# One wait instead of two where a matmul unit's row halves change places, with a new work list

## The chip, the cores and the metric

The kernel runs on one core of a Trainium2 chip. The core has five engines that work side by side, each through its own queue in order: TensorE (PE, matmuls; PEld are its weight loads), VectorE (DVE), ScalarE (ACT), GpSimd (POOL) and SyncE (SP). They meet through semaphores. Matmuls write to PSUM, which DVE and ACT can read; all else lives in SBUF, and DMA queues move data between SBUF and memory (HBM). The metric is the device time of one execution in microseconds, the median of the runs of one kernel.

## The reference

Attention over 8 batches of 8 heads, 576 queries each, with 16 extra "beacon" keys in front that every query sees; the other keys are causal. Its output, as 4608 tokens of 512, goes through a SwiGLU feed-forward block with an inner width of 1536.

```python
k_all = np.concatenate([beacon_k, k], axis=2)          # 592 keys, D = 64
v_all = np.concatenate([beacon_v, v], axis=2)
scores = scale * np.matmul(q, k_all.transpose(0, 1, 3, 2))
scores = np.where(causal, -1000000000.0, scores)
a = np.exp(scores - scores.max(-1, keepdims=True))
a /= a.sum(-1, keepdims=True) + 1e-09
attn_out = np.matmul(a, v_all)                          # (8, 8, 576, 64)
x = attn_out.transpose(0, 2, 1, 3).reshape(4608, 512)
g = x @ w_gate
silu = g * (1.0 / (1.0 + np.exp(-g)))
out = silu * (x @ w_val) @ w_out
```

All inputs and the output are float32; the kernel casts to bf16 as it loads and multiplies in bf16 with float32 sums.

## The kernel before

**Two row halves.** Most matmuls contract over 64 rows only. The array's 128 rows are used as two halves: two matmuls with 64 rows each run at the same time, one in rows 0 to 63, the other in rows 64 to 127, and they write to two different PSUM banks. A unit is one PSUM tile of two banks. In a gate/value unit, for example, rows 0 to 63 first sum the gate into bank 0 while rows 64 to 127 sum the value into bank 1 (piece G, four pairs of matmuls); then the halves change places, rows 64 to 127 finish the gate and rows 0 to 63 the value (piece H, four pairs). Attention-value units (P, then p, 15 pairs each) and projections (24 pieces F of one pair each, of which the first twelve have the first order) do the same. [...] The function `halves` (L112 to L134) issues every such matmul and decides on the wait: it keeps, for each bank of a PSUM slot, the row half that wrote it last, that matmul's name, its place in the order, and a flag that says whether a wait is still owed. A wait is an instruction on TensorE's queue that depends on an earlier matmul; in the built program it hangs on the next weight load. Whatever follows on TensorE stands behind it. With `last` as the latest matmul in either bank of the slot, the test is:

```python
if last[3]:
```

After a wait all flags of the slot are cleared; the matmul issued next sets its own bank's flag. So the first matmul of the new order (rows 64 to 127, bank 0) waits for the last one of the old order, and its partner (rows 0 to 63, bank 1) finds the flag that the first has just set and waits for that one in turn.

**The work list.** There is no loop over the work. A string, `plan` (L610 to L629), names the pieces in the order in which they are issued; each letter calls one function with its own running count (`piece`, L544 to L597), and as every engine takes its queue in order, the string fixes the order on each of them. The letters that matter here:

- `l`: the next load from the list `loads` (L525 to L539), issued on POOL's queue. A load waits until the one eight places earlier has landed, and until its buffer is free. Four loads are issued ahead of the list.
- `c C 0`, `T`, `K k Q q`: for batches 0 to 2, regrouping, transposes on TensorE and copies of k and q; `t`: for batches 3 to 7, a DMA transpose on SP's queue.
- `S` and `s`: scores of one of four parts (A, B, C, D) of a head pair; `s` also adds the causal mask by matmuls. `E`: exponent on ACT.
- `M`, `D`: the causal mask of the next unit that `s` didn't mask, on POOL (L329, an affine select) or on DVE (L325, a product).
- `P`, `p`, `R`: attention-value in both orders, and the division on DVE. The P of a head pair reads the masked exponents of its four parts.
- `X`, `V`: transposes of x, on TensorE for batch 0 and as DMA on SP's queue for the others.
- `g`: the first gate/value unit, in pieces that `parts` (L541) lists; `G`, `H`: the other 107 units. `a`, `1`, `2`: tanh on ACT (L413) and two DVE steps (L417, L424), of which the last frees the PSUM slot.
- `F`: one pair of a projection; `O`, `o`: its copy on DVE or ACT, with the store on SP's queue. `h`, `b`: a few warming matmuls, and a copy of the first beacons.

There are four PSUM slots of two banks (`take`, `give`), taken and given back in turn by scores, attention-value, gate/value units, projections and transposes.

Of the kernel before, what the change touches and what calls it, by code (L numbers as in the profile page):

```python
# [55 lines left out]
def kernel(  # L56
# [55 lines left out]
    def halves(key, bank, row, o, l, r, start, stop, turn=False):  # L112

        at = (held[key], bank)
        was = writers.get(at)
        if was is not None and was[0] != row:
            last = max((w for (i, _), w in writers.items() if i == at[0]), key=lambda w: w[2])
            if last[3]:
                gate = nc.tensor.nop()
                tc.add_manual_dep(  # L120
                    gate.ins,
                    last[1],
                    mybir.DependencyInfo(mybir.DependencyClass.Sync, mybir.DependencyReason.DATA),
                    reason="one bank, two row halves",
                )
            for other, w in writers.items():
                if other[0] == at[0]:
                    writers[other] = (w[0], w[1], w[2], False)
        if turn:
            ins = nc.tensor.transpose(o, l, r)  # L130
        else:
            ins = nc.tensor.matmul(o, lhsT=l, rhs=r, start=start, stop=stop)  # L132
        order[0] += 1
        writers[at] = (row, ins.ins.name, order[0], True)  # L134
# [94 lines left out]
    def turn(n):  # L229
        b, m = divmod(n, NPAIR)  # L230
        t_ps = turned[n] = take(("t", n), [P, 2, 1024], BF16, "t_ps")
        g = grouped.pop(n)
        for i in range(ROWS):
            for row in range(2):
                r = slice(HALF * row, HALF * row + HALF)
                halves(("t", n), row, row, t_ps[:, row, HALF * i : HALF * i + HALF], g[r, i, :], ident[r, r], 1, 1, True)
        if m == 0:
            for mm in range(NPAIR):
                halves(
                    ("t", n), 0, 0, t_ps[:, 0, S + HALF * mm : S + HALF * mm + HALF],  # L240
                    beacons[:, b, P * mm : P * mm + P], ident[0:HALF, 0:HALF], 1, 1, True,
                )
# [19 lines left out]
    def dma_transposes(b):  # L262
        def one(is_k, c, n):
            nc.sync.dma_start_transpose(
                (qT, kT)[is_k][b % 2][:, :, P * c : P * c + n],
                qk[b % 2][0:n, QK * is_k + H * D * c : QK * is_k + H * D * c + H * D],
            )

        todo = []
        for c in range(NKT):  # L270
            todo.append(lambda c=c: one(1, c, P if c < 4 else 80))
            todo.append(lambda c=c: one(0, c, P if c < 4 else 64))
        return todo
# [8 lines left out]
    def scores(n, masked):  # L282
        b, m, u = unit(n)
        ps = take(("s", n), [P, 2, 512], FP32, "s_ps")
        shown[n] = ps, masked
        parts = UNITS[u][2]
        for t, col, q0, w in parts:
            for hh in range(2):
                r = slice(HALF * hh, HALF * hh + HALF)
                halves(  # L290
                    ("s", n), hh, hh, ps[:, hh, col : col + w],
                    kT[b % 2][r, m, P * t : P * t + P], qT[b % 2][r, m, q0 : q0 + w],
                    not masked or col == 0, not masked,
                )
        if masked:
            pieces = []
            for col, w, d in UNITS[u][3]:
                x = d
                while x < d + w:
                    y = min(d + w, (x // HALF + 1) * HALF)  # L300
                    pieces.append((col + x - d, y - x, x // HALF, x % HALF))
                    x = y
            for i, (col, w, g, at) in enumerate(pieces):
                for hh in range(2):
                    r = slice(HALF * hh, HALF * hh + HALF)
                    halves(
                        ("s", n), hh, hh, ps[:, hh, col : col + w],
                        below[r, g, :], ident[r, HALF * hh + at : HALF * hh + at + w],
                        False, i == len(pieces) - 1,
                    )  # L310
# [227 lines left out]
        vl[7][2], vl[7][3], vl[7][4], vl[7][5],  # L538
    ]  # L539
    turns = [load for b in range(NPE, B) for load in dma_transposes(b)]  # L540
    parts = [(0, [(0, 0), (1, 0), (1, 1), (0, 1)], False), (0, [(0, 2), (1, 2)], False), (0, [(1, 3), (0, 3)], True)]  # L541
    wholes = 1

    def piece(kind):  # L544
# [56 lines left out]
    def warm2():  # L601
# [6 lines left out]
        give("heat")  # L608

    plan = [  # L610
        "l0lblTcqKTlkQslEslESclcTESlQTESQMlEsKMKEsMlESEsllPEspMEsRlPEslpEslRXEslYlPEsXlpYEsRlgElXPylplgRl",
        "lXcYTlcgkQlTGaclq1SlHk2lETcGlQaTMHKql1Gkl2aGl1SH2EllSHaDlE1G2laSHE1MS2aGMlE1SH2lEPMSaDlGE1lp2HMR",
        "Gal1SGEl2SHlEDPaDSHE1p2aMSRGE1MH2SGaE1SHME2PaDSFpE1FFRFSFEFF2SFFFEDMFFDFcPcTcpkTQFFkFQTFFqRSFFEF",
        "FKFVSMFEScFFOFlFETlOFFFQSFlESFKFESlFFDESFMDFFFMPEMSFlpEDtSFlESRFFFtFlESDFFPMOEMSplOEGRtlGMDtSHlE",
        "GtlaS1HlEtM2HlatG1Mal2Gtl1H2ltPaSlH1Etp2aMGRG1H2Ha1Ga2G1H2Ga1H2Ha1Ga2G1lH2lHal1SFatFFl2FEFF1FltS",
        "FES2FlFFDtFEDSlPFEFMtplSFRFESlFtEFFDFMSFESMVPlFFEDplFRFFlFFFlFOSFESOFlFESFDFMFESMPlFFEDplSFtRFEF",
        "lFFFDtFFFDFSoOPGEtpDGRtHtGa1H2Ga1H2Ha1Ga2G1H2Gal1Hl2Gal1Hl2Gal1Hl2Hal1Gal2Gl1H2lGal1SHE2HaDS1aFF",
        "F2EFFF1SFEtFS2FESFDMFtFESDPFFtEpDSFRlFFESltFEFDFSlFDFVESFMFPlOoFFEpDlSFRFlEFSFEFDFSFDFEMSPFEFDpS",
        "FRFEStFEFFDFSFtDMESFPFEDtSpFRFEMGtMFGooHtGa1Ht2Gat1H2Gta1Ht2Glal1StHEl2HtaDlG1alt2PlH1tlp2aGRltG",
        "l1HV2lGal1Hl2Gla1Hl2Gla1Hl2Halt1SFaFF2EFtFF1SFMESF2FFFFEDGMGHGa1H2Ha1Ga2FFH12Ga1SFEH2FDaSGE1FF2H",  # L620
        "DSaGE1FFF2FSFDEFSHoMOESGaDGE1H2MGa1H2SaHE1G2aGDH12SHaE1PaF2Fp1SFEFRFFFFSF2ESFFDFDPEDSFtpEMPRSFtE",
        "pFDSRFEPtFFDpDFtRlFFFlFFStoOFlFFESFFlFVFESDFlFESFFMFESDlPFFEDpSFRFEMSFEFFDFSFDESFFFFtEDSFOFFFEOF",
        "FFDMStFEFFFGtMGtHGat1FFFH2Ga1H2Ha1Ga2FFH12Ga1G2HGa1H2Ha1Ga2FFH12Ga1G2HHa1Ga2FFF1PF2FpoOPHRpaSFRE",
        "FFFFF1SFESF2FFFDFEMSFDESFPFEDSpFERSFFFFEFDSVFDESFFDFOFEMSFFOFFEMSFPFEDSpMESFRFFEPFDSMpESFRFFFEMS",
        "FEFMSFFPEMSFpEDGRMGHSHaE1FFaG21FG2HOoHDa1PaG2p1HRGa2VG1H2Ha1Ga2G1H2Ga1H2Ga1H2Ga1H2Ha1Ga2G1H2Ga1H",
        "2Ha1Ga2G1H2Ga1H2Ga1H2Ha1FaFFF2FFG12GHHa1Ga2FFF1G2FFFHGa1H2Ha1Ga2FFF1G2FFFFFFFFFFoFFFoFFFFFFFFHHa",
        "1FaFFF1FFFFFFFFFoOFFFF2FFF2FFFFGGHGa1FFFF2FHGa1H2FaFFG1F2FFFFOoFFFHGa1H2Ha1Ga2FFH12Ga1FFH2FaFFF1",
        "G2GHHa1FaFFF2FFF1FFF2FFFOoFFFFFFFFFFFFFFFFFFFFFFFFoOFFFFFFFFFFFOFFFFFOFFFFFFFOo",
    ]  # L629
    for kind in "".join(plan):  # L630
        piece(kind)
# [38 lines left out]
```

## Time and profile before

| what | us |
|---|---|
| median of 3 runs (423.65 to 427.2) | 424.16 |
| profiled execution, whole time | 425.79 |
| profiled execution, span of its instructions | 424.1 |
| TensorE busy in that span | 391.4 |
| VectorE busy | 233.6 |
| ScalarE busy | 184.6 |
| GpSimd busy | 123.0 |

The span runs from the first to the last instruction. Busy times are sums over an engine's instructions, overlaps counted once. A row of waits names the engine and line that waited, the engine and line that ended the wait, then the sum in us, how often, and the longest one. A row of the timeline has start, duration, engine, line, operation, tiles and the count of instructions in one row; idle time ahead of it stands in brackets, with what ended it. Nearly all matmuls of the program are recorded under L132, so they are told apart by their tiles: gv_ps is gate/value, pv_ps attention-value, o_ps the projection, s_ps scores. In the 40 slices a digit is the busy share in tenths of a slice of 10.6 us, and PEclk is the granted clock of TensorE in the same tenths.

### The profile page before, as it was taken

Reading aid. Unit: us, or ns where it says so; the run is one execution under the profiler, and the core shown is the slowest. Engines: PE = TensorE matmul, PEld = TensorE weight load, DVE = VectorE, ACT = ScalarE, POOL = GpSimd, SP = SyncE. Lnnn points to the kernel's source line nnn. Section 1 sums busy time; section 2 is a strip of 40 time slices with the busy share of each in tenths; the row PEclk is TensorE's granted clock in tenths of the full one; section 3 lists DMA queues with packets and bytes.
Section 4 is the critical chain, followed back from the end, with each engine's and each line's share of the span. In section 5 each row is a group of like instructions: output and inputs, shape, how many; then the busy total and the mean of one; then the engine's idle time right before and its main releaser. Section 6 shows DMA issues by size and latency. Waiting matters only on the chain.

```text
span 424.1 us, 12037 instructions
## 1 busy us (share of the span) xinstructions
PE 391.4 (92%) x5263; PEld 186.5 (44%) x5263; DVE 233.6 (55%) x424; ACT 184.6 (44%) x266; POOL 123.0 (29%) x200
## 2 busy tenths in 40 slices
PE   5889729999999999999999999999999999999996
PEld 2645314554445434544334465335554333333334
DVE  5627606766664567447756655466536666334631
ACT  2925504685346335753337458223852222212210
POOL 8837265178518620562400024000120000000000
PEclk9777959999999999999999999999999999999999
DMA  9999999099999991999931049401222100020112
GB/s 157 171 203 183 203 121 72 2 97 200 135 150 100 179 141 28 113 164 161 154 70 39 12 59 164 109 2 53 37 73 74 32 2 2 2 100 2 51 50 100
DMA packets 143973, 39.92 MB, mean 94 GB/s; under 512 B 130352, under 2 KB 139312, under 8 KB 143920
## 3 DMA queue, kind: packets, MB, share of 16 engines
q0 software_dynamic: 95264, 18.83, 60.6%
q1 hardware_dynamic: 48368, 19.95, 26.5%
q8 instruction: 41, 0.67, 0.7%
q10 hardware_dynamic: 288, 0.36, 0.3%
q14 instruction: 12, 0.10, 0.1%
HBM read 38.27 MB, written 9.44 MB: 113 GB/s over the span
## 4 chain that ended last, share of the span: by engine, by line
PE 83%; DMA 9%; POOL 3%; issue 2%; ACT 1%; DVE 0%; ACTq 0%
PE gv_ps L132 47%; PE o_ps L132 24%; PE pv_ps L132 8%; DMA qk<-in_q_dram 4%; PE s_ps L132 4%; DMA wv<-in_moe_w_val_dram 4%; DMA first<-in_k_dram 1%; POOL p L329 1%; ACT p L316 1%; POOL qk L169 1%; POOL qk L160 0%; PE t_ps L130 0%; POOL wg L200 0%; POOL wv L200 0%; POOL wo L208 0%
## 5 line engine op out<-in xcount | busy, mean ns | idle before, releaser
L132 PE MATMUL gv_ps<-xT,wg 64*128 64x512 bf16 x864 | 218.1, 381 | 0.6 <-ACT p L316 0.2
L132 PE MATMUL gv_ps<-xT,wv 64*128 64x512 bf16 x864 | 200.8, 381 | 8.2
L132 PE MATMUL o_ps<-wo,hT 64*128 64x512 bf16 (+2 forms) x912 | 126.4, 365 | 1.5
L413 ACT ACTIVATE th<-gv_ps 128x512 f32<-128x512 f32 x108 | 64.5, 598 | 144.7 <-PE gv_ps L132 139.9
L417 DVE SCALAR_TENSOR_TENSOR u<-th,gv_ps 128x512 f32<-128x512 f32 x108 | 73.9, 684 | 90.6 <-ACT th L413 90.6
L316 ACT ACTIVATE p<-s_ps 128x992 bf16<-128x992 f32 (+2 forms) x128 | 105.0, 865 | 42.9 <-PE s_ps L132 36.1
L132 PEld LDWEIGHTS <-wv 64*128 64x128 bf16 x864 | 67.3, 94 | 87.8 <-PE gv_ps L132 58.1
L132 PEld LDWEIGHTS <-wg 64*128 64x128 bf16 x864 | 68.7, 94 | 48.5 <-PE gv_ps L132 3.0
L424 DVE SCALAR_TENSOR_TENSOR hT<-gv_ps,u 128x512 bf16<-128x512 f32 x108 | 74.5, 690 | 3.6
L132 PEld LDWEIGHTS <-hT 64*128 64x128 bf16 x912 | 49.9, 94 | 41.9 <-PE o_ps L132 10.2
L329 POOL TENSOR_SCALAR_AFFINE_SELECT p<-p 128x256 bf16<-128x256 bf16 (+2 forms) x67 | 25.2, 394 | 136.5 <-ACT p L316 128.0
L132 PE MATMUL pv_ps<-vb,p 64*128 64x65 bf16 x1920 | 50.1, 192 | 13.9 <-POOL p L329 9.9
L132 PE MATMUL s_ps<-qT,kT 64*128 64x80 bf16 (+4 forms) x384 | 53.7, 290 | 1.8 <-DVE kT L214 1.2
L132 PEld LDWEIGHTS <-p 64*128 64x128 bf16 x1920 | 40.0, 95 | 29.9 <-POOL p L329 10.2
L169 POOL DMA_DIRECT2D vb<-in_v_dram x40 | 34.1, 865 | 17.3 <-DMA qk<-in_q_dram 4.3
L325 DVE TENSOR_TENSOR p<-p,upper 128x256 bf16<-128x256 bf16 (+2 forms) x79 | 20.9, 288 | 20.9 <-ACT p L316 20.4
L132 PEld LDWEIGHTS <-kT 64*128 64x128 bf16 x384 | 25.0, 97 | 15.9 <-issue 2.1
L360 DVE RECIPROCAL rec<-pv_ps 128x10 f32<-128x10 f32 x32 | 7.0, 220 | 42.7 <-PE pv_ps L132 39.2
L361 DVE TENSOR_TENSOR x<-pv_ps,rec 128x640 bf16<-128x640 f32 x32 | 26.4, 824 | 1.2
L214 DVE COPY o_sb<-o_ps 128x512 f32<-128x512 f32 (+2 forms) x23 | 14.6, 658 | 19.2 <-ACT o_sb L212 11.5
L169 POOL DMA_DIRECT2D qk<-in_q_dram x25 | 21.5, 860 | 12.0 <-DMA qT<-qk 9.4
L169 POOL DMA_DIRECT2D qk<-in_k_dram x25 | 21.4, 856 | 11.6 <-DMA kT<-qk 6.1
(46 smaller groups left out, 95.0 us busy)
## 6 DMA issues: line engine op xcount, KB each, us to landing
out_dram<-o_sb SPq DMA_DIRECT2D x34, 256.0 KB, 2.7
vb<-in_v_dram POOLq DMA_DIRECT2D x24, 128.0 KB, 6.9
qk<-in_q_dram POOLq DMA_DIRECT2D x20, 128.0 KB, 7.6
qk<-in_k_dram POOLq DMA_DIRECT2D x15, 128.0 KB, 7.4
wg<-in_moe_w_gate_dram POOLq DMA_DIRECT2D x4, 384.0 KB, 10.0
wv<-in_moe_w_val_dram POOLq DMA_DIRECT2D x4, 384.0 KB, 10.8
wo<-in_moe_w_out_dram POOLq DMA_DIRECT2D x2, 768.0 KB, 12.4
qk<-in_k_dram POOLq DMA_DIRECT2D x2, 576.0 KB, 13.6
```

Source lines behind the costliest of these rows:

```text
L132: ins = nc.tensor.matmul(o, lhsT=l, rhs=r, start=start, stop=stop)
L169: return nc.gpsimd.dma_start(dst[p0 : p0 + n, c, :, 0:D], src[b, :, r : r + n, :].rearrange("h j d -> j h d"))
L214: eng.tensor_copy(o, i)
L316: nc.scalar.activation(pt[n // 4 % NPT][:, :, c0 : c0 + w], ps[:, :, 0:w], ACT.Exp, scale=0.125)
L325: nc.vector.tensor_tensor(out=ap, in0=ap, in1=upper[:, None, d : d + w].to_broadcast([P, 2, w]), op=ALU.mult)
L329: nc.gpsimd.affine_select(out=ap, in_=ap, compare_op=ALU.is_ge, fill=0.0, base=d, pattern=[[0, 2], [1, w]], channel_multiplier=-1,)
L360: nc.vector.reciprocal(rec[:], o[:, :, :, D : D + 1])
L361: nc.vector.tensor_tensor(out=xs[b][:, :, P * m : P * m + P].rearrange("p c (h d) -> p h c d", d=D), in0=o[:, :, :, 0:D], in1=rec[:].to_br ...
L413: nc.scalar.activation(th[:], gvs[n][0][:, 0, :], ACT.Tanh, scale=0.5)
L417: nc.vector.scalar_tensor_tensor(out=u[:], in0=ths[n][:], scalar=1.0, in1=gvs[n][0][:, 0, :], op0=ALU.add, op1=ALU.mult)
L424: nc.vector.scalar_tensor_tensor(out=hTs[j][:, f, :], in0=gvs.pop(n)[0][:, 1, :], scalar=0.5, in1=ths.pop(n)[:], op0=ALU.mult, op1=ALU.mult)
```

## The change

In `halves` the test looks at the flag of the bank that is about to be written (`was`) and no longer at the flag of the latest matmul in the slot (`last`). The first matmul of the new order finds its bank's flag set and waits, for `last` as before; the flags are then cleared, and its partner finds its own bank's flag cleared and doesn't wait. The first wait is for the latest matmul of the old order in either bank.

The first gate/value unit's middle part is split in two, so that `parts` has four entries instead of three and `g` stands four times in the list. The list `loads` stays as it is. The string `plan` is replaced by another: the same pieces, in another order, with some moved to another engine (masks `D`/`M` from 64/52 to 53/60, score units masked by TensorE `s` from 12 to 15, stores `O`/`o` from 23/15 to 21/17, copies `K`/`k` from 6/6 to 9/3 and `Q`/`q` from 8/4 to 6/6, `Y`/`y` from 3/1 to 2/2). The first three lines of each list are given here, the rest is cut. The fifth `P` stands in the second line of both (`H2lEPMSaD` before, `EMSlPaDGl` after).

```diff
         was = writers.get(at)
         if was is not None and was[0] != row:
             last = max((w for (i, _), w in writers.items() if i == at[0]), key=lambda w: w[2])
-            if last[3]:
+            if was[3]:
                 gate = nc.tensor.nop()
...
-    parts = [(0, [(0, 0), (1, 0), (1, 1), (0, 1)], False), (0, [(0, 2), (1, 2)], False), (0, [(1, 3), (0, 3)], True)]
+    parts = [(0, [(0, 0), (1, 0)], False), (0, [(1, 1), (0, 1)], False), (0, [(0, 2), (1, 2)], False), (0, [(1, 3), (0, 3)], True)]
...
     plan = [
-        "l0lblTcqKTlkQslEslESclcTESlQTESQMlEsKMKEsMlESEsllPEspMEsRlPEslpEslRXEslYlPEsXlpYEsRlgElXPylplgRl",
-        "lXcYTlcgkQlTGaclq1SlHk2lETcGlQaTMHKql1Gkl2aGl1SH2EllSHaDlE1G2laSHE1MS2aGMlE1SH2lEPMSaDlGE1lp2HMR",
-        "Gal1SGEl2SHlEDPaDSHE1p2aMSRGE1MH2SGaE1SHME2PaDSFpE1FFRFSFEFF2SFFFEDMFFDFcPcTcpkTQFFkFQTFFqRSFFEF",
...
+        "0lllbTclkQTlKqslEslcEscTlKTEslKEslQEslQlEslEslPEslpEsRPllpEsXRlESElYsXEMsglEslEsPElplyPRlgplXRll",
+        "YXglcylcTgkQlTGcalKqTHlKqG1la2SHE1S2aMGE1G2MSHcElTHaMKqGl1a2SlHE1MSaG2lE1SlH2EMSlPaDGlE1p2lHRlSG",
+        "aEM1SHE2MlSaDGlE1SH2EMSPaMGE1pM2SHERPaGD1p2HRSFaFFEF1SFF2FEMSFFFcFEMFcTFMTqKFPqKSFEpcSFRFEMTFtFF",
...
     ]
```

## The prediction

> **What bounds the kernel now.** I read the page's table of engines and its 40 slices first:
>
> ```profile
> PE 391.4 (92%) x5263; PEld 186.5 (44%) x5263; DVE 233.6 (55%) x424; ACT 184.6 (44%) x266; POOL 123.0 (29%) x200
> PE   5889729999999999999999999999999999999996
> PEclk9777959999999999999999999999999999999999
> DMA  9999999099999991999931049401222100020112
> ```
>
> TensorE is busy in every slice but the sixth (about 53 to 64 us), and the next engine has 55%. The chain that ended last gives PE 83% of the span. So what TensorE waits for, inside its own stream, is the price list. The view of waits has, for TensorE:
>
> ```profile
> PEld L132 <- PE gv_ps L132: 63.4, 121, 0.6
> PEld L132 <- PE o_ps L132: 10.5, 25, 0.6
> PEld L132 <- PE pv_ps L132: 9.3, 28, 0.6
> PE pv_ps L132 <- POOL p L329: 9.9, 2, 9.7
> ```
>
> Three of the four are TensorE waiting for itself; the first, in the timeline of PE inside a stretch of gate/value units:
>
> ```profile
> 204.08 0.38 PE L132 MATMUL gv_ps<-xT,wg 64*128 64x512 bf16 x2
> 204.54 0.39 PE L132 MATMUL gv_ps<-xT,wv 64*128 64x512 bf16 x1
> 204.54 0.39 PE L132 MATMUL gv_ps<-xT,wg 64*128 64x512 bf16 x1
> 204.76 0.38 PE L132 MATMUL gv_ps<-xT,wv 64*128 64x512 bf16 x1
> ...
> 206.06 0.38 PE L132 MATMUL gv_ps<-xT,wg 64*128 64x512 bf16 x2
> 206.51 0.39 PE L132 MATMUL gv_ps<-xT,wv 64*128 64x512 bf16 x1
> ```
>
> Pairs of matmuls, one per row half, start 0.215 us apart (204.54 to 204.76), but once in each unit the step is 0.45 (206.06 to 206.51). A unit takes 206.51 - 204.54 = 1.97 us for eight pairs that need 8 x 0.2155 = 1.725: 0.245 is lost. The place is the change of row halves, where the first matmul of the new order must end before its partner may start.
>
> **The second waits, counted and priced.** In the instruction order of both kernels, weight loads of row half 0 into bank 1 that wait for TensorE number 160 before (109 gate/value, 32 attention-value, 19 projection) and none after. Each kernel keeps the first wait. Start to start over the whole trace, 107 G pieces have a mean of 0.875 us and 107 H pieces 1.106, the same eight matmuls: again about 0.24. For a projection I take 0.245 too: it has the shape of the gate matmuls (64x512). Attention-value has small matmuls:
>
> ```profile
> 178.27 0.63 PE L132 MATMUL pv_ps<-vb,p 64*128 64x65 bf16 x30
> 178.72 0.61 PE L132 MATMUL o_ps<-wo,hT 64*128 64x512 bf16 x4
> 179.17 0.87 PE L132 MATMUL pv_ps<-vb,p 64*128 64x65 bf16 x30
> ```
>
> Thirty of them take 0.63 in the first order and 0.87 in the changed one: 0.24 each.
> Here the Trainium skill (page "TensorE: Matmul & The Clock Gate", section "Single matmul latency") would give less. By it a matmul alone takes (398 + N)/2.4 ns, 379 ns at N = 512, which is this trace's 381; against the step of 216 a waited matmul would cost an estimated 0.163 us, as the page counts no signalling. The rule makes 120 large waits worth 19.6 us, the row 29.4. I take the row, since it contains the semaphore.
>
> **What of it lies under another stall.** The sixth slice holds one wait of 9.7 us. The timeline of POOL, then PE's restart:
>
> ```profile
> 51.95 0.73 POOL L169 DMA_DIRECT2D vb<-in_v_dram  x1 [4.04 <-DMA wo<-in_moe_w_out_dram]
> 57.53 0.83 POOL L169 DMA_DIRECT2D qk<-in_k_dram  x1 [2.54 <-DMA qk<-in_q_dram]
> 58.35 0.89 POOL L169 DMA_DIRECT2D qk<-in_q_dram  x1
> 59.23 0.90 POOL L169 DMA_DIRECT2D qk<-in_k_dram  x1
> 60.11 1.06 POOL L329 TENSOR_SCALAR_AFFINE_SELECT p<-p 128x256 bf16<-128x256 bf16 x3
> ...
> 60.60 0.40 PE L132 MATMUL pv_ps<-vb,p 64*128 64x65 bf16 x8 [9.67 <-POOL p L329]
> ```
>
> The fifth P (batch 1, first head pair) needs masks that POOL makes, and POOL takes its queue in order: they stand behind load issues, each of which waits until the load eight places ahead has landed (in the chain, the 576 KB q load of batch 2 runs from its issue at 38.41 for 18.84 us, to 57.25; the issue at 57.53 follows). In the new list the last mask that this P needs stands behind the 36th `l` instead of the 37th, one issue of 0.9 earlier, and the load list is the same. So P may begin at 58.35 + 0.89 + 0.35 = 59.6 instead of 60.60, and without the second pause (its last 12 matmuls began at 61.23 before): the next gate unit starts about 1.5 us sooner. Six H and four p stand ahead of that P in both lists, so the eight gate/value and four attention-value waits there (12 x 0.24 = 2.9 us) only lengthen the stall: they earn nothing. What hides them is the load; were it gone, they would count.
> Could that load land sooner? By my sum of shapes, loads up to it read 19.04 MB from HBM by 57.25, begun at 1.31: 340 GB/s. The skill's page "DMA: Bandwidth & Descriptors" (section Specifications) puts a core's HBM limit at about 358 GB/s: an estimate of 53.2 us for the same bytes, so at best 3 us sooner. By the row nothing. I take nothing.
>
> **The sum.** Behind the fifth P lie 101 gate/value, 28 attention-value and 19 projection waits: 101 x 0.245 = 24.7, 28 x 0.24 = 6.7, 19 x 0.245 = 4.7, together 36.1 us. With 1.5 from the mask: 37.6. TensorE works almost without a gap from then on (windows from 70, 215 and 320 us: busy 140.2 of 145 us, 101.7 of 105, 97.5 of 104), so each comes off the span unless something new is late.
>
> **What the rest costs.** (a) First waits now stand by themselves: about 77 that an earlier second wait covered are explicit. Bounds: nothing, if the unit's last matmul has long ended, and 0.245 each (19 us), the price of a wait just behind. The latter needs less than 0.44 us of other work between; in the new list eight places have that little (ten before), so I take 0. Queued behind a waiting weight load is all of TensorE; ACT's tanh would wait for it next. (b) Three more score units are masked by TensorE: 16 matmuls more, all ahead of the stall, which hides them (else about 0.4 us at the small-matmul steps). Splitting the first unit's middle part adds no matmul. (c) Masks go from 64 on DVE and 52 on POOL to 53 and 60, and some copies change between DVE and ACT: 11 x 0.29 us less DVE, 8 x 0.39 more POOL, both far from full. (d) Loads, transposes and output stores move with the list. I laid the new list out at 0.863 for G and H, 0.2155 for F, 0.46 for P and p, 0.09 to 0.21 for S, beginning at 59.6. The list's 45th to 106th load, issued at 87 to 201 us before, fall at about 86 to 172 us. That is tight, for DMA was idle only near 160 to 170 of that window. But batch 7's scores stand at about 269, so even the 109 busy microseconds of before, ending near 195, cover them. Masks between the 79th and the 95th load have 28 us until their P; those between the 62nd and the 78th only 2 us and more, which is the place of rival 4. On SP's queue the transposes of x stand 8 to 10 us ahead of the first G that reads them, in both. (e) Small new waits for ACT, DVE and slots: before, G's mean exceeds its 0.863 by 0.012, so 107 units lost 1.3 us in all; bounds 0 and the rival below; I take 1.5.
> Span: 424.1 - 37.6 + 1.5 = 388.0. The profiled execution took 425.79, the median of three is 424.16, as near to the span as runs go (423.65 to 427.2), so I give 388 for the time.
>
> **The rivals.**
> 1. Forecast, 383 to 393: 0.66.
> 2. The early stall goes too: other timing of the first loads lets the masks through. For: the list was laid against landings. Against: queue order and bytes above. It would give back up to 10 us: 377. 0.08.
> 3. Slots become the bound. A unit holds its PSUM slot for four pieces of 0.863, 0.17 of drain, then 0.60 + 0.68 + 0.69 and some 0.2 of handing over: 5.8 us. Four slots at 1.73 per unit give 6.9; with one held by an open projection three give 5.2, so 0.2 us per unit are lost; on half of the units 10 us, on all 20: 398 to 408. For: the faster TensorE leaves no slack. Against: by the same sum three slots were short before (6.3 against 5.9), and G lost 0.012. 0.18.
> 4. Slower: POOL's masks stand behind loads in the dense attention too. The 28 later P would each have to wait over (37.6 + 4.2)/28 = 1.5 us, as the fifth did for 9.7. For: loads now come packed into 86 us. Against: both waits in the row for POOL above lie before 62 us, and after it there is none. From 429: 0.05.
> 5. The rewrite doesn't remove the waits, or gains and losses meet within 1%: 0.03. The order of instructions speaks against it.
>
> **How the numbers follow.** Range 377 to 399: the forecast's case, the second, and the near half of the third. About 1% is what a measurement tells from no change here. Faster by over 1% has cases 1 to 3, 0.92; within 1% 0.03; slower 0.05.
>
> **What would show it.** H pieces at 0.86 to 0.88 start to start, units at 1.73, p at 0.63; waits of weight loads for gv_ps, o_ps and pv_ps shrunk to a fraction of 83 us; still one stall of 11 to 12 us ending near 59.5 on POOL's mask; TensorE's busy count lower in time but its share after 62 us still over 95%. Wrong would be: H at 0.86 but new gaps ahead of G (slots) or of P (masks), or H still near 1.1.

## The result, and the profile after

The changed kernel takes 394.14 us, the median of four executions (390.53 to 396.55), against 425.0 for the kernel before on the same chip (423.65 to 427.2, four executions): a ratio of 0.924, interval 0.915 to 0.933. The forecast was 388. The profile below is of the slowest of the four executions, 396.55 us with a span of 394.8, which the ratio leaves out as it lies over 1.5% above the fastest.

The page after: the table of engines, then the 40 slices (of 9.9 us each).

```profile
PE 361.8 (92%) x5279; PEld 206.9 (52%) x5279; DVE 230.6 (58%) x412; ACT 182.3 (46%) x268; POOL 125.7 (32%) x206
PE   5949929999999699999996999999999999999996
PEclk8695978999999789999999999999999999999999
DMA  9999999269999999995499204981051200010112
```

TensorE is still the only engine near its limit, and its busy time fell by 29.6 us, as much as the span (29.3). The stall of the sixth slice is still there, one of about 5 us stands in the third slice, and two are new, in the fourteenth (around 133 us) and the twenty-second (around 212). Beside the fourteenth the granted clock is down to 0.7.

The view of waits, TensorE's rows that answer to those of before, and a new one:

```profile
PE pv_ps L132 <- POOL p L329: 9.7, 3, 4.6
PE gv_ps L132 <- DMA xT<-x: 6.7, 2, 3.7
PEld L132 <- PE gv_ps L132: 3.3, 8, 0.6
PEld L132 <- PE o_ps L132: 1.4, 4, 0.6
PEld L132 <- PE pv_ps L132: 0.4, 2, 0.2
```

TensorE's waits for its own gate/value, projection and attention-value matmuls were 63.4 + 10.5 + 9.3 = 83.2 us in 174 places; now they are 5.1 us in 14. What remains are first waits that have too little work in front of them. The row for the transposes of x (6.7 us in two places) is new.

A stretch of gate/value work in the timeline of PE:

```profile
140.68 0.38 PE L132 MATMUL gv_ps<-xT,wg 64*128 64x512 bf16 x1
...
141.54 0.38 PE L132 MATMUL gv_ps<-xT,wg 64*128 64x512 bf16 x1
141.56 0.58 PE L132 MATMUL gv_ps<-xT,wv 64*128 64x512 bf16 x2
141.77 0.38 PE L132 MATMUL gv_ps<-xT,wg 64*128 64x512 bf16 x1
...
143.49 0.62 PE L132 MATMUL pv_ps<-vb,p 64*128 64x65 bf16 x30
```

Thirteen pairs between 140.68 and 143.49 are 0.216 us apart, with changes of the row halves among them, as at 141.54 to 141.77: the step of 0.45 is gone. From the start of one piece to the start of the next, in us, with the median of one piece and the sum over the whole trace (a pause is counted to the piece ahead of it):

| piece | median before | after | sum before | after |
|---|---|---|---|---|
| G | 0.863 | 0.863 | 93.7 | 95.4 |
| H | 1.110 | 0.863 | 118.4 | 95.2 |
| P | 0.498 | 0.455 | 28.5 | 33.9 |
| p | 0.745 | 0.450 | 26.5 | 18.8 |
| F | | | 100.6 | 98.2 |

Together -26.2 us, of which H is 23.2 and p 7.7. (Neighbouring pieces overlap at their edges, so a sum is good to about 1 us, that of F to 3.) G and P have grown, P by 5.4, though its median fell: the pauses at 23.7 and at 131 us, told of below, lie in or behind a P.

**The early stall.** PE around it, then POOL:

```profile
51.94 0.62 PE L132 MATMUL pv_ps<-vb,p 64*128 64x65 bf16 x10 [0.66 <-POOL p L329]
54.66 0.29 PE L132 MATMUL pv_ps<-vb,p 64*128 64x65 bf16 x8 [2.09 <-DMA qk<-in_q_dram]
59.33 0.51 PE L132 MATMUL pv_ps<-vb,p 64*128 64x65 bf16 x12 [4.38 <-POOL p L329]
```
```profile
57.13 0.83 POOL L169 DMA_DIRECT2D qk<-in_k_dram  x1 [2.26 <-DMA qk<-in_q_dram]
...
58.84 0.43 POOL L329 TENSOR_SCALAR_AFFINE_SELECT p<-p 128x256 bf16<-128x256 bf16 x1
```

As forecast, the last mask of the fifth P stands behind a load issue that waits until a q load has landed (57.13, before 57.53), and P's last part starts at 59.33. But TensorE reaches this P at 51.3 and not at 47.5, mainly because the first P with a mask made by POOL already waits 4.6 us, from 23.9 on, behind another load. So the stall here is 7.1 us in three parts (0.66 + 2.09 + 4.38), and it ends where it was forecast to end.

**The new stalls.** PE around the first of them, the queue of SP ahead of it, and three windows (length, then the busy time of PE, PEld, DVE, ACT and POOL, the granted clock, the DMA share, GB/s; the share is the packets' time over that of 16 engines and can exceed 1):

```profile
130.88 0.62 PE L132 MATMUL pv_ps<-vb,p 64*128 64x65 bf16 x30
135.15 0.58 PE L132 MATMUL gv_ps<-xT,wg 64*128 64x512 bf16 x1 [3.65 <-DMA xT<-x]
135.15 0.60 PE L132 MATMUL gv_ps<-xT,wv 64*128 64x512 bf16 x1
135.53 0.63 PE L132 MATMUL gv_ps<-xT,wg 64*128 64x512 bf16 x1
```
```profile
121.33 7.53 SPq L385 DMA_TRANSPOSE xT<-x  x5
```
```profile
70.00:215.00 145.00, 135.98 (x2258) 79.24 (x2254) 92.75 (x178) 80.06 (x113) 68.00 (x104) 0.98 1.51 122
135.00:140.00 5.00, 4.85 (x52) 2.63 (x54) 1.25 (x3) 0.73 (x2) 3.42 (x5) 0.50 1.45 225
215.00:220.00 5.00, 5.00 (x34) 2.31 (x31) 0.25 (x1) 0.60 (x1) 0.00 (x0) 0.66 0.46 138
```

SP takes 7.53 us to issue one batch's five transposes of x, from 121.33 on, and the first G that reads them comes to its turn at 131.3, ten us after the first issue. It starts at 135.15. The same happens at 211.3 (six transposes issued from 205.76 in 9.10 us).

Before, the same five took 7.43 us to issue, from 129.96 on, and G came 10.8 us after the first issue, without a wait:

```profile
140.80 0.38 PE L132 MATMUL gv_ps<-xT,wv 64*128 64x512 bf16 x1
```

So the distance shrank by less than 1 us there. What grew is the time of each transpose from its issue to its landing, in the view of xT before (129 to 142 us) and after (120 to 136 us):

```profile
L385 SPq DMA_TRANSPOSE xT<-x x5: 1185/1266/2227, 130.0 to 136.1; - x5
DMA to landing us min/median/max: 4.2/4.9/5.9
```
```profile
L385 SPq DMA_TRANSPOSE xT<-x x5: 1212/1283/2168, 121.3 to 127.6; - x5
DMA to landing us min/median/max: 7.8/8.0/8.0
```

The DMA share from the first issue to the end of the landing was 1.74 before (129.96 to 139.50) and 2.49 after (121.33 to 135.10). At the second place it is the other way round: landing takes a median of 5.0 us before and 5.2 after, but the distance from the first issue to G's turn fell from 7.8 us (206.18 to 213.94) to 5.5.

After each of these pauses the matmuls are 0.40 instead of 0.216 us apart for some microseconds: the granted clock is 0.50 and 0.66 in the two windows. At these clocks 4.85 busy us do the work of about 2.4, and 5.00 that of 3.3: an estimate of 2.4 + 1.7 us lost beside the waits themselves.

In the long window TensorE is busy for 135.98 of 145 us, 93.8%, where the forecast had over 95%; in the one after it, from 215 to 320 us, for 104.00 of 105.

Counted from the first gate unit after the early stall (62.0 before, 59.65 after) to the end of the span, the kernel took 362.1 us before and takes 335.2 now: 26.9 us of the 36.1 came through.

### The profile page after: what moved, and what is told of

Same layout as the page of the kernel before. It is cut to its first block, busy times and chain, and to the rows that moved or that the text cites. A ratio compares the mean times of both kernels' runs of the same rounds, so it can differ in the third digit from the quotient of the medians.

```text
span 394.8 us, 12065 instructions
## 1 busy us (share of the span) xinstructions
PE 361.8 (92%) x5279; PEld 206.9 (52%) x5279; DVE 230.6 (58%) x412; ACT 182.3 (46%) x268; POOL 125.7 (32%) x206
## 4 chain that ended last, share of the span: by engine, by line
PE 75%; DMA 15%; POOL 4%; issue 2%; ACT 2%; DVE 1%; SPq 1%; POOLq 0%; ACTq 0%
PE gv_ps L132 45%; PE o_ps L132 21%; PE pv_ps L132 5%; DMA qk<-in_q_dram 5%; DMA xT<-x 4%; PE s_ps L132 4%; DMA wv<-in_moe_w_val_dram 4%; DMA wg<-in_moe_w_gate_dram 2%; SPq L385 1%; POOL vb L169 1%; DVE o_sb L214 1%; POOL qk L160 1%; ACT o_sb L212 1%; ACT p L316 1%; POOL qk L169 0%
## 5 line engine op out<-in xcount | busy, mean ns | idle before, releaser
L132 PE MATMUL gv_ps<-xT,wg 64*128 64x512 bf16 x864 | 204.4, 384 | 8.5 <-DMA xT<-x 6.7
L132 PE MATMUL gv_ps<-xT,wv 64*128 64x512 bf16 x864 | 205.2, 384 | 0.0
L132 PE MATMUL o_ps<-wo,hT 64*128 64x512 bf16 (+2 forms) x912 | 116.5, 365 | 0.2
L132 PEld LDWEIGHTS <-wg 64*128 64x128 bf16 x864 | 80.9, 95 | 55.9 <-issue 11.2
L132 PEld LDWEIGHTS <-wv 64*128 64x128 bf16 x864 | 80.4, 95 | 41.6 <-issue 3.1
L329 POOL TENSOR_SCALAR_AFFINE_SELECT p<-p 128x256 bf16<-128x256 bf16 (+2 forms) x73 | 27.9, 400 | 129.8 <-ACT p L316 127.0
L132 PEld LDWEIGHTS <-hT 64*128 64x128 bf16 x912 | 46.6, 94 | 32.9 <-PE o_ps L132 1.4
L132 PE MATMUL pv_ps<-vb,p 64*128 64x65 bf16 x1920 | 43.4, 195 | 13.7 <-POOL p L329 9.7
L132 PE MATMUL s_ps<-qT,kT 64*128 64x80 bf16 (+4 forms) x384 | 46.7, 289 | 2.8 <-ACT p L316 1.1
L169 POOL DMA_DIRECT2D vb<-in_v_dram x40 | 33.9, 856 | 20.5 <-DMA qk<-in_q_dram 6.7
L325 DVE TENSOR_TENSOR p<-p,upper 128x256 bf16<-128x256 bf16 (+2 forms) x69 | 18.0, 284 | 18.1 <-ACT p L316 17.7
L361 DVE TENSOR_TENSOR x<-pv_ps,rec 128x640 bf16<-128x640 f32 x32 | 26.4, 824 | 1.2
```

What stands on the lines that cost most here:

```text
L169: return nc.gpsimd.dma_start(dst[p0 : p0 + n, c, :, 0:D], src[b, :, r : r + n, :].rearrange("h j d -> j h d"))
L325: nc.vector.tensor_tensor(out=ap, in0=ap, in1=upper[:, None, d : d + w].to_broadcast([P, 2, w]), op=ALU.mult)
L329: nc.gpsimd.affine_select(out=ap, in_=ap, compare_op=ALU.is_ge, fill=0.0, base=d, pattern=[[0, 2], [1, w]], channel_multiplier=-1,)
L361: nc.vector.tensor_tensor(out=xs[b][:, :, P * m : P * m + P].rearrange("p c (h d) -> p h c d", d=D), in0=o[:, :, :, 0:D], in1=rec[:].to_br ...
```

## The experiments

**The list alone, and the waits alone.** The theory: the second waits are the gain, and the new list by itself does nothing. The rival: a good part comes from the list.

The new list with the old test:

```diff
-            if was[3]:
+            if last[3]:
```

> The new work list and parts, with the old test, so every second wait is back. If the waits are the gain, it takes 420 to 428 us, about as the kernel before: it wins the 1.5 us at the early mask, and the two new waits for transposed x (3.65 and 3.0 us in the profile after) shrink because the units arrive later. If the list is worth something by itself, under 415.

Measured 425.39 us (423.7 to 427.21, ten executions) beside 424.85, ratio 1.001, interval 0.998 to 1.003. The view of waits has the second waits back at their old price:

```profile
PEld L132 <- PE gv_ps L132: 61.0, 117, 0.6
```

The old list and the old `parts` with the new test:

```diff
-            if last[3]:
+            if was[3]:
```

> The old work list and the old parts of the first unit, with the new test for the wait alone. If the removed waits are the gain (my sum: 36.1 us behind the fifth P), it takes 386 to 394 us, H pieces fall from 1.106 to about 0.865 us, and the early stall still ends near 60.6 us because the last mask still stands behind the 37th load. If the new list is what pays, or if the old list runs into new waits of its own once TensorE is faster, it stays above 400.

Measured 398.49 us (397.4 to 400.44) beside 424.85, ratio 0.938, interval 0.933 to 0.942. It lies between what the two theories gave, a few us worse than the waits alone should do. H has a median of 0.863 here too, so the waits came out as priced, and the early stall has grown from 9.9 to 14.8 us:

```profile
PE pv_ps L132 <- POOL p L329: 14.8, 2, 14.6
```

It now lasts from 44.4 to 59.2: TensorE gets to the fifth P earlier, and the mask comes when the load lets it. That explains why what is won ahead of the stall earns nothing, but not the few us, for the 36.1 lay behind it. There 26.2 us came through (from the first gate unit after the stall, at 60.52, to the end 335.9 us instead of 362.1), about as in the changed kernel. So the shortfall behind the stall is there with the old list too: the view of waits has 5.5 us for x in three places, and 4.8 us in four pauses of attention-value that wait for nothing.

The waits alone give 26.4 us, the list alone nothing, and both together about 31. In the run of the list alone TensorE's waits for POOL's masks fell from 9.9 to 4.7 us, but one of 2.6 us for x is new; the sum is what it was.

**The price of the second waits by kind of unit.** In the new kernel, the second waits put back for attention-value and projection only:

```diff
-            if was[3]:
+            if was[3] or (key[0] != "g" and last[3]):
```

> The changed kernel with the second wait back for attention-value and projection, and left out for gate/value alone. By the prices of the prediction, 28 x 0.24 + 19 x 0.245 = 11.4 us come back: 404 to 407 us. If the small attention-value waits lie under other pauses (masks, or TensorE's own supply of instructions), only the projections count and it is about 399.

Measured 402.82 us (398.98 to 404.83), ratio 0.942, interval 0.935 to 0.949. On the same chip a kernel that differs from the changed one only by 32 tiny matmul pairs at its start, told of below, took 392.89. So the 47 waits behind the early stall (and four ahead of it) are worth about 9.9 us, to within some 3.5 by the two intervals; the sum had 6.7 + 4.7 = 11.4. The median of p goes back from 0.450 to 0.724.

**The early stall.** Is it really POOL's queue, and what is it worth? First, in the changed kernel the masks of the first nine units are taken to DVE (eight letters `M` become `D`):

```diff
-        "aEM1SHE2MlSaDGlE1SH2EMSPaMGE1p...
+        "aED1SHE2DlSaDGlE1SH2EMSPaMGE1p...
```

> The changed kernel with the first nine masks all on DVE instead of POOL, so that none of them stands behind a load. If POOL's queue order alone makes the early stalls (4.8 us at 24 us and 7.7 us between 51 and 59 us in the profile after), the fifth P starts by about 51 us and the time falls by 7 to 12 us, to 380 to 386. If the landing of loads holds TensorE up elsewhere early on, less than 3 us are won.

A miss: 391.56 us (389.1 to 394.41), ratio 0.921, interval 0.914 to 0.928, within the error of the changed kernel's. The fifth P now starts at 47.9 without a stall, but the sixth stops for 6.95 us from 57.9 on. The timeline of POOL shows why:

```profile
63.62 0.79 POOL L169 DMA_DIRECT2D qk<-in_q_dram  x1
64.32 1.49 POOL L329 TENSOR_SCALAR_AFFINE_SELECT p<-p 128x256 bf16<-128x256 bf16 x4
```

The next mask runs at 64.32 only, right behind ten load issues of which the first waited for a landing until 56.01. The stall had moved on to the first mask that was left on POOL. So the same was done with the masks of the first 17 units (14 letters), among them:

```diff
-        ...EF1SFF2FEMSFFFcFEMFcTFMTqKF...
+        ...EF1SFF2FEDSFFFcFEDFcTFDTqKF...
```

> The changed kernel with all seventeen masks up to batch 1's end on DVE, so that no mask stands among the loads issued up to about 67 us. If POOL's queue order is the whole of the early stall, the 7.0 us pause that only moved on to the sixth P in the run with nine masks (57.9 to 64.9 us) goes as well: first F at 64 to 67 us instead of 73, 383 to 388 us in all. If what TensorE lacks there is loaded data, the pause stays in some other wait and the time stays at 390 to 394.

Measured 381.34 us (379.16 to 383.51) beside 427.68, ratio 0.894, interval 0.889 to 0.900. No wait of TensorE for POOL is left, the first F starts at 58.9 instead of 73.1, and DVE can take the work:

```profile
50.00:60.00 10.00, 10.00 (x206) 5.77 (x206) 8.91 (x20) 6.77 (x11) 5.37 (x7) 1.00 1.82 166
```

TensorE is busy for the whole ten us in which it stood still before, at full clock, with DVE at 8.91 of 10. Against the changed kernel this is a further 3% (0.894 to 0.924), some 13 us.

**The waits with the stall out of the way, in the old list.** The old list with the first 20 units masked by DVE (13 letters), once with both waits and once with the new test. In the list of both, for example:

```diff
-        ...QTESQMlEsKMKEsMlESE...
+        ...QTESQDlEsKDKEsDlESE...
```

With both waits, then with one:

> The kernel before with its first twenty masks on DVE and both waits kept. If POOL's queue order alone makes the stall of 9.9 us at 50.8 us, 8 to 10 us are won: 0.976 to 0.982 of the kernel before. If the loads themselves are late, less than 3 us: above 0.992.

> The old work list with the new test and with its first twenty masks on DVE. If the early stall (14.8 us in the run of the new test with the old list) was POOL's queue order there too, and swallowed some 4 us of what the removed waits had earned, this takes 0.900 to 0.915 of the kernel before, so that the new list is worth no more than 2% once the masks are out of the way. If the old list lacks loaded data at that place, it stays above 0.925.

Measured on one chip beside 426.35: 415.38 us with both waits (410.82 to 416.76; ratio 0.974, interval 0.967 to 0.980) and 380.8 with one (380.27 to 381.34; 0.894, interval 0.891 to 0.897). The first came out at the edge of what was expected, the second better than expected. Three things follow. The early stall costs the kernel before about 11 us. The removed waits are worth 415.38 - 380.8 = 34.6 us, to within some 3, where nothing ahead swallows them; 36.1 and the 2.9 that lay ahead of the stall make 39.0. And the old list with the masks moved (0.894) equals the new one with the masks moved (0.894): of the new list no gain is left over that shows. The missing 4.4 us, not far outside the error, have a likely place in the view of waits. With both waits, TensorE waits 1.9 us for x; with one:

```profile
PE gv_ps L132 <- DMA xT<-x: 6.5, 3, 4.2
```

In the old list too, a faster TensorE comes too early for x. The same run has two stretches of half clock that the one with both waits lacks (3.41 us each, from 110.0 and 188.5), so how the 4.4 us divide is not shown.

**The transposes of x.** In the changed kernel, those of batches 2 and 4 were issued right behind the division that completes their x, ahead of the transposes of q and k that stood in front of them (`V` moved up to its `R` in two places):

```diff
-...lFEtFlFFRSFlFEtSFEDFMSFlFVFEDSF...
+...lFEtFlFFRVSFlFEtSFEDFMSFlFFEDSF...
```

> The changed kernel with the DMA transposes of x for batches 2 and 4 moved up in the list to just behind the R that completes their x, ahead of one and of two or three transposes of k and q on SP's queue. If SP's queue order makes the two waits for x (at 131 and 211 us in the profile after), they shrink by 2 to 4 us each and, with no long pause, the clock doesn't fall behind them: 385 to 390. If the DMA engines are the limit (their share was above 2 there), x lands no sooner and the time stays within 391 to 395.

Measured 392.49 us (391.5 to 393.64), ratio 0.924, interval 0.919 to 0.929. No gain that shows. The wait at 131 is gone and the one at 211 is down to 2.2 us, but a pause that waits for nothing in the profile stands at the same place:

```profile
132.94 0.63 PE L132 MATMUL pv_ps<-vb,p 64*128 64x65 bf16 x30
135.83 0.27 PE L132 MATMUL s_ps<-qT,kT 64*128 64x208 bf16 x2 [2.27 <-issue]
```

Next, instead of moving x forward, six v loads that share the DMA engines with it were moved back, in among the gate/value units of batch 2 (six letters `l`):

```diff
-        ...FFEOSFlFFDFlEDSFESDFlFFPEMSFlpEDPRlFFplSDF...
+        ...FFEOSFFFDFEDSFESDFFFPEMSFpEDPRFFpSDF...
...
-        ...REGtaD1Gt2HGta1PHt2patGRH1VGa2lH1l2G...
+        ...REGtaD1Gt2HlGta1PHlt2patGlRHl1VGla2lHl1l2G...
```

> The changed kernel with the six v loads of batch 4 (needed only by the P at about 180 us) moved behind the first gate units of batch 2's chunk, so that they no longer run together with the transposes of x before it. If the share of the DMA engines makes x late there (2.6 to 2.9 between 126 and 135 us), the 3.65 us wait for x at 131 us falls below 1.5 us, the clock stays up behind it, and 3 to 6 us are won: 388 to 391. If SP's queue order alone sets it, the wait stays above 3 us and the time at 392 to 395.

A miss: 398.18 us (393.17 to 401.15), ratio 0.928, interval 0.920 to 0.937. The wait at 131 went, but x was late at 157.0 (1.5 us) and at 210.2 (4.8 us), 6.5 us in all, nearly as before. These two runs don't separate whether x lands late because it is issued late on SP's queue or because DMA is full (the share in the window from 131 to 135 us is 2.87); the second shows only that moving loads about moves the wait about. The views of xT above say more: at 131 the landing took longer, at 211 the issue stood too close.

**The pauses that wait for nothing.** In the changed kernel there are two, at 126.75 and 253.03 us, each about 1 us, in the middle of attention-value pieces. Counted along TensorE's instructions they stop ahead of number 3778 and number 7363: 194 and 195 beyond a multiple of 256. The page has a DMA queue called instruction with 41 packets and 0.67 MB, so 16 KB each; 41 x 256 = 10,496 is nearly the 10,601 instructions of TensorE in the trace. The theory: instructions come in blocks of 256, and TensorE ran through one block before the next was there. The rival: something about these very matmuls. To shift all that follows by 64 instructions, 32 tiny matmuls with their weight loads were put in at the start:

```diff
     warm(6, P)
+    warm(32, 16)
```

> The changed kernel with 32 pairs of weight load and matmul of 16 columns (64 instructions of TensorE) put among the first warming ones, where TensorE waits for its first data anyway. The pauses of 1 us without any wait, at 126.8 and 253.0 us in the profile after, lie at TensorE's instructions 3778 and 7363, both 194 or 195 more than a multiple of 256. If they come from the fetch of instructions in blocks of 256, they are seen again at 194 or 195 beyond a multiple of 256 in the new count, which is 32 matmuls earlier in the work, and not at the old matmuls. If they belong to the work that stands there, they stay at the same matmuls, 64 further in the count. The time stays within 2 us of the changed kernel.

Measured 392.89 us (392.13 to 393.59), ratio 0.920, interval 0.915 to 0.924. The pauses left the old matmuls and went to numbers 4290, 6339 and 7362 of the new count, which are again 194, 195 and 194 beyond a multiple of 256. One of them:

```profile
249.10 0.63 PE L132 MATMUL pv_ps<-vb,p 64*128 64x65 bf16 x29
250.47 0.19 PE L132 MATMUL pv_ps<-vb,p 64*128 64x65 bf16 x1 [0.75 <-issue]
```

The theory holds; why the place is 194 and not 0 stays open. In the other kernels every longer pause of this kind, in the dense part, lies at such a number as well, and TensorE goes on 2.3 to 3.1 us after a packet of that queue began. It also explains the run with x ahead: its pauses stand at 3778 and at 4034, one block later. In the changed kernel TensorE had been waiting for x just ahead of the second of these, and the wait gave the fetch its time. With x early, the fetch was the next thing to be late.

**What the runs point to.** The masks of the first 17 units on DVE, x of batches 2 and 4 ahead, and four transposes `t` moved behind the latter's `V`. The last, in one line:

```diff
-        "RPEFFptDSFRESFFFtFEMSFFFFEtOSFoFPDMESFtpFERlSFFtlFESFDFFDlFVESD...
+        "RPEFFpDSFRESFFFFEMSFFFFEOSFoFPDMESFpFERVtlStFFttltFESFDFFDlFESD...
```

> The seventeen masks on DVE, the transposes of x for batches 2 and 4 just behind the R that completes their x, and four DMA transposes of q and k (the 34th to 37th) behind those of batch 4. If the second wait for x (3.1 us at 196 us in the run with seventeen masks) is one of SP's queue order, it falls below 1 us and the time is 0.880 to 0.891 of the kernel before. If the DMA engines or the supply of instructions fill the place, it stays at 0.892 to 0.897.

Measured 377.14 us (376.84 to 378.02, six executions) beside 426.35, ratio 0.886, interval 0.883 to 0.888: the fastest kernel here, 11.4% below the kernel before and some 4% below the changed one. Waits for x are down to 3.1 us in three places, none longer than 2.2, and after the third slice the granted clock is never below 0.8 of full.

## Why the prediction was right, and where it was off

The path and the price were right: TensorE's own second waits came off the span for the greater part (26.9 of 36.1 us in the changed kernel, 34.6 of 39.0 where the stall was gone too). The time of 394.14 us lies just above the forecast's own case (383 to 393) and inside the range only since that reached into the case of the slots, which did not happen; that much is luck.

- **The second waits: right, in place and price.** H fell to 0.863, so 0.247 for each against 0.245. For attention-value 0.24 was too low where pieces stand alone (p fell by 0.295), and with the projections the runs gave 9.9 of 11.4 us, within the error. The whole of it came out at 34.6 of 39.0 with the stall out of the way.
- **First waits standing alone at nothing: right** but for the eight gate/value and six other places that show 5.1 us in the view of waits, where twelve and more such waits stood before.
- **The early stall: its mechanism and its end were right** (59.33 where 59.6 was said), its length was not, since the arrival at the fifth P was put 3.8 us too early: a stall on the first POOL mask, at 23.9 us, was overlooked. It costs nothing more, because the load sets the end. That the list alone is worth nothing fits.
- **What it is worth to be rid of the stall** was put at up to 10 us. The runs gave 11 with the old waits and about 13 with the new ones, by taking masks off POOL's queue.
- **The term that was off is (d).** "On SP's queue the transposes of x stand 8 to 10 us ahead of the first G that reads them, in both" was taken as time enough and priced at nothing. In the kernel before it was 10.8 and 7.8 us at the two places, and only just enough: the last transposes that the two G read landed at 139.50 and 213.81, 1.3 and 0.1 us ahead of them. So there was hardly any slack to lose. After, 10.0 us are left at the first place, where a transpose lands 8.0 instead of 4.9 us after its issue, and 5.5 us at the second, where the issue of six alone takes 9.10. That cost 6.7 us of waits, 0.9 in a small one at 91 us (the view names a copy on ACT there, and x in the run with seventeen masks), and about 4.1 for the clock that fell after the pauses. These 11.7 us are the shortfall of 9.2 (36.1 - 26.9) and more.
- **The allowance (e) of 1.5 us** did not foresee the supply of instructions, 2.1 us. With 11.7 this makes 13.8 named us against a shortfall of 9.2. About 4.6 us of small gains lie in that stretch which I can't place one by one; p alone, at 0.295 for 28 pieces instead of 0.24, is 1.5 of them.
- **The forecast by its parts:** the gate unit came at 59.65 instead of 60.5 (0.85 early), the rest of the span took 335.2 instead of 327.5 (7.7 late): 394.8 instead of 388.0.
- **The rivals.** Slots as the bound: not seen, G kept its 0.863, and one gate/value unit waits 0.7 us for a projection's copy, at 334.5. POOL's masks behind loads in the dense attention: not seen; they stayed where they had been, in the first 60 us. The rewrite without effect: refuted by the instruction order and by the rows.

What stays open is why the transposes of x took 8.0 instead of 4.9 us to land at the first place: the DMA share was higher, but no run changes that alone. Nor does any run leave out the first wait, which the code explains as "one bank, two row halves", so what it guards is not shown here.

## What to carry to other kernels

When TensorE gets faster, lay out every producer that feeds it against the new times, not only the engine that the change touches: here the transposes of x, counted from their first issue through their own issue time to the landing, had 10.8 and 7.8 us with hardly any to spare, and were left with 10.0 and 5.5. A compute step on a queue that also issues loads inherits the landing of a load eight places ahead; it helps little to move some of such steps, for the stall goes on to the next one that was left behind. And a pause of TensorE can cost about half as much again as the wait itself, when the clock comes down behind it (here an estimated 4.1 us beside 6.7).

## What was not expected of the hardware

- TensorE's instructions are fetched in blocks of 256, and where matmuls are small enough (an attention-value piece of 60 instructions takes 0.45 us, so a block would last 1.9) the next block is not there in time. Pauses of 0.5 to 3 us lie 194 or 195 instructions beyond a multiple of 256 in all kernels here. The kernel before had one such pause, at 22.6 us (1.5 us); with the same list and the new test there are four, of 0.9 to 2.2 us. So the waits that were taken out had given the fetch its time.
- The clock comes down by windows of time, not by the length of a pause. In every trace the granted clock is either full or half, and it changes only on a fixed grid of 3.41 us: in the changed kernel it is half for 6.83 us from 133.73 on and for 3.41 us from 215.65 on. Two waits for x, the first in the run with the attention-value and projection waits put back, the second in the one with 32 tiny matmul pairs, each with the grid windows around it (columns as above):

```profile
217.01 0.58 PE L132 MATMUL gv_ps<-xT,wg 64*128 64x512 bf16 x1 [1.71 <-DMA xT<-x]
213.59:217.00 3.41, 1.64 (x49) 0.86 (x42) 1.88 (x6) 1.84 (x3) 0.00 (x0) 1.00 1.52 144
217.00:220.41 3.41, 3.40 (x18) 1.40 (x20) 0.00 (x0) 0.00 (x0) 0.00 (x0) 0.50 0.88 234
```
```profile
131.90 0.37 PE L132 MATMUL gv_ps<-xT,wg 64*128 64x512 bf16 x1 [3.10 <-DMA xT<-x]
130.03:133.44 3.41, 1.54 (x42) 1.14 (x44) 0.00 (x1) 0.00 (x0) 3.41 (x6) 1.00 1.71 220
133.44:136.86 3.42, 3.42 (x36) 1.93 (x32) 2.62 (x5) 1.11 (x2) 2.09 (x4) 1.00 1.91 193
```

  The wait of 1.71 us lies in one window, and the next window runs at half clock. The wait of 3.10 us is divided between two windows, and the clock stays. Counted from one matmul's start to the next, in all kernels here between 60 us and the end: each of the 13 full-clock windows with 2.07 us or more of pause was followed by one at half clock, and none with up to 2.06 was (twelve had 1.7 to 2.06). In the first 60 us two windows with 1.85 and 1.91 us, and smaller pauses beside, were followed by half clock too, so the one long pause is not the whole measure. The Trainium skill (page "TensorE: Matmul & The Clock Gate", section "What's actually happening") has the clock come down after at least one idle window of about 3.4 us, in a window that runs freely. The grid agrees; the idle time does not, for 2.07 us of a window was enough. The four executions of the changed kernel differ in the clock too: the fastest (390.53 us) has a mean of 0.982, the slowest (396.55) 0.952. That this comes from where their pauses fell in the grid is not shown, since one of them alone was traced.
